# A recurrence in chunks and two feed-forward layers on one core: half 1's chunks in swapped rows, small products of both halves in turn, and one subtraction of layer 2 on VectorE

## The chip, the cores and the metric

The kernel runs as one program on one core of a Trainium2 chip. The metric is the device time of one execution in microseconds, smaller is better. Three executions of the kernel before were timed; one more was profiled.

## What is computed

The first part is a recurrence over 768 steps for 4 batches of 8 heads, with a state of 40 x 40 for each head; two feed-forward layers follow on its 3072 rows of 320 numbers.

```python
for t in range(768):
    y[t] = einsum('bhd,bhde->bhe', r[t], state)
    Sa = einsum('bhde,bhe->bhd', state, a[t])
    state = state * w[t][..., None] - einsum('bhd,bhe->bhde', Sa, b[t]) + einsum('bhd,bhe->bhde', v[t], k[t])
x = y as rows of 8 heads x 40                     # 3072 x 320
x = square(maximum(x @ w_in, 0)) @ w_out          # layer 1, 320 -> 2048 -> 320
h = x @ w_in2;  out = (h - tanh(h)) @ w_out2      # layer 2
```

All inputs and outputs are float32; the weights of the layers reach the chip as float64 bits and are converted there.

## The kernel before

**Attention.** The sequence is cut into 6 stretches of 128 steps, the batches into two pairs, so that there are 12 items k (`NT`). Of an item's two batches each is a half j (0 or 1). Inside the 128 steps there are two blocks (`blk`) of 64, and each block has two chunks (`c2`) of 32; c = 0..3 numbers the four chunks. Four pairs of heads lie beside each other in rows 0 to 39 and 64 to 103. `scalings` (L170) multiplies the decays up by scans on VectorE. `front` (L229) and `solve` (L292) build and invert the small triangular systems of two items at once on VectorE. `keys` (L259) transposes the scaled keys on TensorE, and ScalarE copies them from PSUM to `kbn`: a chunk takes 64 rows (32 of k, 32 of b), chunk 0 of a block rows 0 to 63 and chunk 1 rows 64 to 127.

`back` (L334) is the recurrence. For each chunk c, one after the other:

1. at a block's first chunk the state `zi` is transposed into `pz` (L393), 16 instructions (a float32 product shows as two instructions in the trace);
2. `pu` (L399): 8 products per half with 104 rows of contraction and 32 columns of the array, all 8 at columns `r0 = 64 * c2 + 32`, the same for both halves;
3. ScalarE writes -`pu` into the tile `vu` (L401), and copies `pz` to `zt` (L405);
4. `pd` (L423): 8 products per half from 64 rows `k0 = 64 * c2`, the outputs in turn in columns 0 to 39 and 64 to 103 (`par`);
5. VectorE adds `pd` to the state (L428, two instructions per half), at the last chunk it also multiplies by the decay (L430).

In steps 2 and 4 the source goes over half 0 first and then over half 1, each with a PSUM tile of its own. `result` (L435) makes the outputs from `vu`: transposed (L443), scores `pm` (L451) masked by a constant from `cst` (L454), and products with `kbn` and `zt` (L469, L472). `b_load` (L323) loads v into rows `64 * c2` and following of `vu`, and `v_load` (L164) loads v into `zi`.

**Layers.** `stream` (L726) runs 12 jobs of 256 rows for layer 1 and 12 for layer 2. A job has 8 steps m: 16 products into `hp` (L789), the activation, and 12 products into `acc` (L738: 8 with the high part `gh` of the activation, 4 with the low part `gl`), these up to 3 steps later. In layer 2, `act2` (L855) of step m issues on ScalarE a square, tanh, relu and square (L857 to L860), then `act2_end` of step m-1 on VectorE (L847, L848), then L863 and L864 of step m on VectorE, then `act2_round` (L850) of step m-1: `gh` on ScalarE (L852) and the subtraction `gl = d - gh` on GpSimd (L853). `split` (L706) prepares the next job's input on GpSimd (L710, L713, L714). Layer 1's own subtraction is on GpSimd as well (L817).

**What sets the order.** The parts are generators that `mix` (L521) walks along a model clock; `clk.run(...)` is what a piece is planned to take on TensorE and `L_E` what comes between two pieces. This gives the program order, and `urgent` gives `back` a higher priority (`HP_B`) than `front` and both a higher one than the layers. A scheduler of the framework then places the instructions on each engine by priority and modelled readiness; on the chip each engine keeps that order. Within one PSUM tile, products keep the order of the source. The attention's PSUM tiles share 4 buffers (`ps_a`), which layer 2 uses for `hp`.

Of the kernel before, what the change touches and what calls it, by code (L numbers as in the profile page):

```python
# [9 lines left out]
F32 = mybir.dt.float32  # L10
# [4 lines left out]
ACTF = mybir.ActivationFunctionType  # L15
ALU = mybir.AluOpType
# [7 lines left out]
C_LM, C_AM, C_ZERO, C_ID = 0, 32, 96, 224  # L24
# [33 lines left out]
def consts():  # L58
    c = np.zeros((128, NCONST), np.float32)
    c[:, C_ID:C_ID + 128] = np.eye(128)  # L60
    i = np.arange(128)
    c[:, C_LM:C_LM + 32] = i[None, :32] < i[:, None] % 32
    rows = (i // 64) * 32 + i % 32
    c[:, C_AM:C_AM + 64] = rows[:, None] < np.arange(64)[None, :]
    return c
# [23 lines left out]
class Attention:  # L89
# [169 lines left out]
    def keys(self, k, j):  # L259
# [4 lines left out]
        q = 2 * (k % 2) + j  # L264
        yield lambda: max(self.s_ready[k][j], self.y_ready[k - 2] - L_Y if k > 1 else 0)
        for blk in range(2):
            pt = self.ps.tile([128, 4, 104], F32, tag="a", name="pt")
            for pr in range(4):
                nc.tensor.transpose(pt[:, pr, :], kbf[0:P, pr, blk, :], self.id[0:P, 0:P])
# [53 lines left out]
    def b_load(self, k):  # L323
# [3 lines left out]
        for j in range(2):  # L327
            q = 2 * (k % 2) + j
            for c2 in range(2):
                (getattr(nc, Q_B) if k else nc.sync).dma_start(out=self.vu[j][64 * c2:64 * c2 + 32, :, :, :, 0:40], in_=vn[s, q, c2])  # L330
# [3 lines left out]
    def back(self, k):  # L334
# [48 lines left out]
        for c in range(4):  # L383
            blk, c2 = c // 2, c % 2
            yield max(ready)
            for j in range(2):
                q = 2 * (k % 2) + j
                zi, vu, zt, au = self.zi[q][:, c2], self.vu[j], self.zt[j], aus[j]
                if c2 == 0:
                    pz = self.ps.tile([128, 4, 40], F32, tag="a", name="pz")  # L390
                    for pr in range(4):
# [4 lines left out]
                r0 = 64 * c2 + 32  # L396
                pu = self.ps.tile([128, 8, 40], F32, tag="a", name="pu")
                for h in range(8):
                    nc.tensor.matmul(pu[r0:r0 + 32, h, :], lhsT=au[0:104, 4 * (h % 2) + h // 2, 32 * c:32 * c + 32],  # L399
                                     rhs=zi[0:104, h % 2, h // 2, :], start=True, stop=True, tile_position=(0, r0))  # L400
                nc.scalar.activation(out=vu[r0:r0 + 32, blk].rearrange("p a r d -> p (a r) d")[:, :, 0:40], in_=pu[r0:r0 + 32],  # L401
                                     func=ACTF.Copy, scale=-1.0)
                if c2 == 0:
                    for p0 in (0, 64):
                        nc.scalar.activation(out=zt[p0:p0 + 40, blk], in_=pz[p0:p0 + 40].rearrange("p a d -> p (a d)"), func=ACTF.Copy)  # L405
# [4 lines left out]
                clk.run(0.28)  # L410
                ready[j] = clk.t + L_E
                if c2:
                    self.u_ready[k][j][blk] = ready[j]
            yield max(ready)
            for j in range(2):
                q = 2 * (k % 2) + j
                vu, kbn, zi, wx = self.vu[j], self.kbn[q], self.zi[q], self.wx[2 * (k and (k - 1) % 3 + 1) + j]
                k0 = 64 * c2
                pd = self.ps.tile([128, 4, 40], F32, tag="a", name="pd")
                for pr in range(4):  # L420
                    for par in range(2):
                        hh = 4 * par + pr
                        nc.tensor.matmul(pd[64 * par:64 * par + 40, pr, :], lhsT=kbn[k0:k0 + 64, blk, 40 * hh:40 * hh + 40],  # L423
                                         rhs=vu[k0:k0 + 64, blk, pr, par, 0:40], start=True, stop=True)
# [6 lines left out]
                clk.run(0.4)  # L431
# [3 lines left out]
    def result(self, k):  # L435
# [12 lines left out]
        def scores(j, blk, vut):  # L448
            pm = self.ps.tile([128, 4, 2, 64], F32, tag="a", name="pm")
            for pr in range(4):  # L450
# [4 lines left out]
                                    in1=cst[:, None, C_AM:C_AM + 64].to_broadcast([128, 8, 64]), op=ALU.mult)  # L455
# [208 lines left out]
def attn_moe(ctx, tc, r, k, v, w, a, b, wakb, w0, rt, vn, vz, w_in1, w_out1, w_in2, w_out2, cst, out):  # L664
# [471 lines left out]
```

## Time and profile before

| what | us |
|---|---|
| three executions | 1388.30, 1394.27, 1395.91 |
| their median | 1394.27 |
| the profiled execution's own time | 1393.79 |
| its span from first to last instruction | 1391.6 |

Over the span TensorE is busy 1221.7 us (88%), VectorE 947.2 us (68%), ScalarE 830.0 us (60%), GpSimd 675.2 us (49%); the granted TensorE clock is 0.941 of full speed in the mean. Up to 105 us the inputs are loaded and the first items prepared. From there to some 985 us the attention's items and layer 1's jobs share TensorE, and from 985 us to the end layer 2 runs.

How to read the rows: PE is TensorE's products, PEld its weight loads, DVE VectorE, ACT ScalarE, POOL GpSimd, SP the engine that issues most transfers. A row of the timeline gives the start in us, the time until the last of its instructions ended in us, engine, line, operation, output<-inputs, shapes, count, and in brackets idle time before it and who ended it. Products overlap each other's ends, so the time that a run of them takes of TensorE is read from its start to the start of the next row, not from the second column. L12 is line 12 of the kernel.

### The profile page before, as it was taken

Reading aid. Unit: us, or ns where it says so; the run is one execution under the profiler, and the core shown is the slowest. Engines: PE = TensorE matmul, PEld = TensorE weight load, DVE = VectorE, ACT = ScalarE, POOL = GpSimd, SP = SyncE. Lnnn points to the kernel's source line nnn. Section 1 sums busy time; section 2 is a strip of 40 time slices with the busy share of each in tenths; the row PEclk is TensorE's granted clock in tenths of the full one; section 3 lists DMA queues with packets and bytes.
Section 4 is the critical chain, followed back from the end, with each engine's and each line's share of the span. In section 5 each row is a group of like instructions: output and inputs, shape, how many; then the busy total and the mean of one; then the engine's idle time right before and its main releaser. Section 6 shows DMA issues by size and latency. Waiting matters only on the chain.

```text
span 1391.6 us, 40716 instructions
## 1 busy us (share of the span) xinstructions
PE 1221.7 (88%) x16682; PEld 1136.5 (82%) x16682; DVE 947.2 (68%) x1812; ACT 830.0 (60%) x1768; POOL 675.2 (49%) x713
## 2 busy tenths in 40 slices
PE   1347778999799988999799999999899999999996
PEld 1246668888789877888788889999899999999995
DVE  7899785555854675356935671321269999999996
ACT  4364627574466736574465746544477777777785
POOL 5366534445444635245533643245555555555543
PEclk9986868989999988999999999999999999999999
DMA  6444544554545535454554534236920000000000
GB/s 159 114 122 143 157 150 136 154 171 137 163 138 164 170 103 161 133 157 132 160 159 134 159 103 147 85 110 217 391 72 19 24 31 22 22 22 22 22 11 22
DMA packets 94406, 164.12 MB, mean 118 GB/s; under 512 B 17696, under 2 KB 66272, under 8 KB 94212
## 3 DMA queue, kind: packets, MB, share of 16 engines
q1 hardware_dynamic: 65028, 124.02, 29.8%
q0 software_dynamic: 9600, 21.68, 5.1%
q10 hardware_dynamic: 19584, 15.74, 3.4%
q8 instruction: 134, 2.20, 0.7%
q14 instruction: 60, 0.49, 0.1%
HBM read 133.81 MB, written 27.53 MB: 116 GB/s over the span
## 4 chain that ended last, share of the span: by engine, by line
DVE 35%; PE 32%; issue 11%; ACT 10%; DMA 8%; POOL 4%; ACTq 0%; SPq 0%; POOLq 0%; DVEq 0%
DVE e L847 10%; PE hp L789 8%; PE acc L738 7%; DVE e L863 4%; DVE e L864 4%; PE pu L399 3%; DVE wx L192 3%; DMA raw<-in_moe_w_in_dram 2%; PE pd L423 2%; PE pm L451 2%; DVE inw L196 2%; PE pa L375 2%; ACT tbd L369 2%; DMA raw<-in_moe_w_out_dram 2%; DVE T L313 1%
## 5 line engine op out<-in xcount | busy, mean ns | idle before, releaser
L853 POOL TENSOR_TENSOR gl<-e,gh 128x512 fp32r<-128x512 f32 x96 | 144.3, 1504 | 180.5 <-ACT gh L852 178.3
L817 POOL TENSOR_TENSOR gl<-g,gh 128x512 fp32r<-128x512 f32 x96 | 127.0, 1323 | 177.4 <-ACT g L816 172.2
L789 PE MATMUL hp<-xh,wi 128*128 128x256 f32 x960 | 195.5, 299 | 12.3 <-ACT r L814 9.9
L789 PE MATMUL hp<-xh,wi2s 128*128 128x256 f32 x960 | 170.0, 278 | 1.7 <-DMA wi2s<-wi 1.7
L789 PEld LDWEIGHTS hp<-xh,wi 128*128 128x128 f32 x960 | 155.7, 202 | 15.7 <-ACT r L814 10.9
L847 DVE SCALAR_TENSOR_TENSOR e<-e,e 128x512 f32<-128x512 f32 x96 | 155.9, 1624 | 3.3
L738 PE MATMUL acc<-wo,gh 128*128 128x320 f32 x768 | 147.2, 327 | 3.1 <-DMA wo<-wo 2.8
L789 PEld LDWEIGHTS hp<-xh,wi2s 128*128 128x128 f32 x960 | 141.9, 188 | 1.9 <-DMA wi2s<-wi 1.9
L789 PE MATMUL hp<-xl,wi 128*128 128x256 f32 x576 | 134.9, 298 | 0.0
L738 PEld LDWEIGHTS acc<-wo,gh 128*128 128x128 f32 x768 | 121.5, 199 | 5.5 <-ACT gh L852 3.0
L428 DVE TENSOR_TENSOR zi<-pd,zi 40x160 f32<-40x160 f32 x192 | 61.8, 322 | 90.4 <-PE pd L423 86.0
L789 PE MATMUL hp<-xl,wi2s 128*128 128x256 f32 x576 | 120.7, 278 | 0.0
L852 ACT ACTIVATE gh<-e 128x512 fp32r<-128x512 f32 x96 | 60.8, 633 | 88.6 <-DVE e L848 86.4
L585 POOL TENSOR_TENSOR st<-hc,st 128x160 fp32r<-128x160 f32 (+3 forms) x72 | 51.6, 717 | 112.7 <-ACT st L584 82.3
L789 PEld LDWEIGHTS hp<-xl,wi 128*128 128x128 f32 x576 | 103.2, 203 | 0.7
L863 DVE TENSOR_TENSOR e<-hp,e 128x512 f32<-128x512 f32 x96 | 65.0, 677 | 54.4 <-ACT e L858 48.9
L476 POOL DMA_DIRECT2D yT<-yt x96 | 65.2, 682 | 71.9 <-DVE yt L475 69.7
L814 ACT ACTIVATE r<-hp 128x512 f32<-128x512 f32 x96 | 57.3, 597 | 66.7 <-PE hp L789 65.0
L789 PEld LDWEIGHTS hp<-xl,wi2s 128*128 128x128 f32 x576 | 94.5, 188 | 0.0
L578 DVE TENSOR_SCALAR hc<-hc 128x160 f32<-128x160 f32 (+3 forms) x78 | 29.2, 375 | 94.9 <-ACT hc L569 87.1
L848 DVE COPY_PREDICATED e<-e,e 128x512 f32<-128x512 int32 x96 | 89.6, 933 | 3.2
L399 PE MATMUL pu<-zi,au 104*32 104x40 f32 x1536 | 79.0, 209 | 11.1 <-DVE zi L428 8.4
(154 smaller groups left out, 3151.4 us busy)
## 6 DMA issues: line engine op xcount, KB each, us to landing
wo<-wo SPq DMA_DIRECT2D x96, 640.0 KB
inq<-in_wakb_dram SPq DMA_DIRECT2D x36, 240.0 KB
raw<-in_moe_w_in_dram SPq DMA_DIRECT2D x24, 256.0 KB
raw<-in_moe_w_out_dram SPq DMA_DIRECT2D x16, 320.0 KB
wo<-st ACTq DMA_DIRECT2D x32, 160.0 KB
wi<-st ACTq DMA_DIRECT2D x40, 128.0 KB
raw<-in_moe_w_out_dram SPq DMA_DIRECT2D x32, 160.0 KB
wo<-st ACTq DMA_DIRECT2D x64, 80.0 KB
```

The costliest lines, as they stand in the source:

```text
L399: nc.tensor.matmul(pu[r0:r0 + 32, h, :], lhsT=au[0:104, 4 * (h % 2) + h // 2, 32 * c:32 * c + 32], rhs=zi[0:104, h % 2, h // 2, :], start= ...
L428: nc.vector.tensor_tensor(out=zn, in0=pd[rows], in1=zi[rows, c2, par], op=ALU.add)
L476: getattr(nc, Q_Y).dma_start(out=self.yT[k].rearrange("(a r d) (b t) -> b r d a t", a=4, r=2, b=2)[j, par][:, :, t], in_=yt[rows])
L738: nc.tensor.matmul(acc[n][j], lhsT=g[:, i, 128 * j:128 * j + 128], rhs=w[:, p, i, :], start=(m == 0 and i == 0 and e == 0), stop=(m == 7 a ...
L789: nc.tensor.matmul(hp[:, h, :], lhsT=wt, rhs=xx, start=(e == 0), stop=(e == 7))
L814: nc.scalar.activation(out=r, in_=hp, func=ACTF.Relu)
L817: nc.gpsimd.tensor_tensor(out=gl, in0=g, in1=gh.bitcast(F32), op=ALU.subtract)
L847: nc.vector.scalar_tensor_tensor(out=u, in0=q, scalar=rest, in1=u, op0=ALU.add, op1=ALU.mult)
L848: nc.vector.copy_predicated(out=d, mask=v.bitcast(I32), data=u)
L852: nc.scalar.activation(out=gh, in_=d, func=ACTF.Copy)
L853: nc.gpsimd.tensor_tensor(out=gl, in0=d, in1=gh.bitcast(F32), op=ALU.subtract)
L863: nc.vector.tensor_tensor(out=d, in0=hp, in1=th, op=ALU.subtract)
```

## The change

It has two parts.

The first is in the attention. In half 1 the two chunks of a block change places in the 128 rows: `b_load` puts them at `64 * (c2 ^ j)`, the mask in `cst` gets a second version rolled by 64 rows, and `keys` of half 1 writes the two chunks to the other place: a transpose in place of which two products with the identity stand, one per 64 columns. In `back` the two halves' 8 `pu` products go into one PSUM tile and alternate, half 0 and half 1 in columns `r0[j] = 64 * (c2 ^ j) + 32`; the two halves' `pd` products alternate too, half 0 and half 1 from different 64 rows and, neighbour by neighbour, into different columns. ScalarE writes both halves' `vu` first and the `zt` copies afterwards; the model times in `clk.run` are other ones.

The second is in layer 2: the subtraction `gl` of `act2_round` is on VectorE in place of GpSimd.

```diff
-C_LM, C_AM, C_ZERO, C_ID = 0, 32, 96, 224
+C_LM, C_AM, C_ZERO, C_ID = 0, 32, 160, 288
@@ consts
+    c[:, C_AM + 64:C_AM + 128] = np.roll(c[:, C_AM:C_AM + 64], 64, axis=0)
@@ keys
-                nc.tensor.transpose(pt[:, pr, :], kbf[0:P, pr, blk, :], self.id[0:P, 0:P])
+                if j:
+                    for c in (0, 64):
+                        nc.tensor.matmul(pt[64 - c:128 - c, pr, :], lhsT=kbf[0:P, pr, blk, c:c + 64], rhs=self.id[0:P, 0:P], start=True, stop=True)
+                else:
+                    nc.tensor.transpose(pt[:, pr, :], kbf[0:P, pr, blk, :], self.id[0:P, 0:P])
@@ b_load
-                ...dma_start(out=self.vu[j][64 * c2:64 * c2 + 32, :, :, :, 0:40], in_=vn[s, q, c2])
+                ...dma_start(out=self.vu[j][64 * (c2 ^ j):64 * (c2 ^ j) + 32, :, :, :, 0:40], in_=vn[s, q, c2])
@@ back
-            for j in range(2):
-                q = 2 * (k % 2) + j
-                zi, vu, zt, au = self.zi[q][:, c2], self.vu[j], self.zt[j], aus[j]
-                if c2 == 0:
+            zis = [self.zi[2 * (k % 2) + j][:, c2] for j in range(2)]
+            if c2 == 0:
+                pzs = []
+                for zi in zis:
                     pz = self.ps.tile([128, 4, 40], F32, tag="a", name="pz")
+                    pzs.append(pz)
...
-                r0 = 64 * c2 + 32
-                pu = self.ps.tile([128, 8, 40], F32, tag="a", name="pu")
-                for h in range(8):
-                    nc.tensor.matmul(pu[r0:r0 + 32, h, :], lhsT=au[0:104, 4 * (h % 2) + h // 2, 32 * c:32 * c + 32],
-                                     rhs=zi[0:104, h % 2, h // 2, :], start=True, stop=True, tile_position=(0, r0))
-                nc.scalar.activation(out=vu[r0:r0 + 32, blk]..., in_=pu[r0:r0 + 32], func=ACTF.Copy, scale=-1.0)
+            pu = self.ps.tile([128, 8, 40], F32, tag="a", name="pu")
+            r0 = [64 * (c2 ^ j) + 32 for j in range(2)]
+            for h in range(8):
+                for j in range(2):
+                    nc.tensor.matmul(pu[r0[j]:r0[j] + 32, h, :], lhsT=aus[j][0:104, 4 * (h % 2) + h // 2, 32 * c:32 * c + 32],
+                                     rhs=zis[j][0:104, h % 2, h // 2, :], start=True, stop=True, tile_position=(0, r0[j]))
+            clk.run(0.4)
+            for j in range(2):
+                q, vu, zt = 2 * (k % 2) + j, self.vu[j], self.zt[j]
+                nc.scalar.activation(out=vu[r0[j]:r0[j] + 32, blk]..., in_=pu[r0[j]:r0[j] + 32], func=ACTF.Copy, scale=-1.0)
...
-            for j in range(2):
-                k0 = 64 * c2
-                pd = self.ps.tile([128, 4, 40], F32, tag="a", name="pd")
-                for pr in range(4):
-                    for par in range(2):
-                        hh = 4 * par + pr
-                        nc.tensor.matmul(pd[64 * par:64 * par + 40, pr, :], lhsT=kbn[k0:k0 + 64, blk, 40 * hh:40 * hh + 40],
-                                         rhs=vu[k0:k0 + 64, blk, pr, par, 0:40], start=True, stop=True)
+            pds = [self.ps.tile([128, 4, 40], F32, tag="a", name="pd") for _ in range(2)]
+            for pr in range(4):
+                for j, par in ((0, 0), (1, 1), (0, 1), (1, 0)):
+                    k0, hh = 64 * (c2 ^ j), 4 * par + pr
+                    nc.tensor.matmul(pds[j][64 * par:64 * par + 40, pr, :], lhsT=self.kbn[2 * (k % 2) + j][k0:k0 + 64, blk, 40 * hh:40 * hh + 40],
+                                     rhs=self.vu[j][k0:k0 + 64, blk, pr, par, 0:40], start=True, stop=True)
+            clk.run(0.5)
@@ scores
-                                    in1=cst[:, None, C_AM:C_AM + 64].to_broadcast([128, 8, 64]), op=ALU.mult)
+                                    in1=cst[:, None, C_AM + 64 * j:C_AM + 64 * j + 64].to_broadcast([128, 8, 64]), op=ALU.mult)
@@ act2_round
-        nc.gpsimd.tensor_tensor(out=gl, in0=d, in1=gh.bitcast(F32), op=ALU.subtract)
+        nc.vector.tensor_tensor(out=gl, in0=d, in1=gh.bitcast(F32), op=ALU.subtract)
```

## Rows read from the trace of the kernel before

**Rows 1.** Stretches: length; busy us of PE, PEld, DVE, ACT, POOL; granted clock; DMA.
```profile
105.00:245.00 140.00, 108.63 (x1976) 96.81 (x1969) 108.45 (x254) 72.58 (x171) 70.63 (x80) 0.74 0.48 146
...
815.00:985.00 170.00, 166.51 (x2491) 157.03 (x2489) 48.92 (x146) 88.93 (x184) 76.59 (x118) 1.00 0.47 152
...
1104.00:1392.00 288.00, 270.65 (x2002) 260.97 (x2000) 271.41 (x290) 208.82 (x378) 141.67 (x96) 0.99 0.07 22
```

**Rows 2.** Timeline of layer 2, two steps and one meeting with `split`.
```profile
1156.02 1.52 POOL L853 TENSOR_TENSOR gl<-e,gh 128x512 fp32r<-128x512 f32 x1 [2.15 <-ACT gh L852]
...
1156.42 1.67 DVE L847 SCALAR_TENSOR_TENSOR e<-e,e 128x512 f32<-128x512 f32 x1
...
1158.12 0.76 DVE L848 COPY_PREDICATED e<-e,e 128x512 f32<-128x512 int32 x1
...
1158.77 0.67 DVE L863 TENSOR_TENSOR e<-hp,e 128x512 f32<-128x512 f32 x1
...
1158.97 0.63 ACT L852 ACTIVATE gh<-e 128x512 fp32r<-128x512 f32 x1 [0.84 <-DVE e L848]
...
1159.37 0.68 DVE L864 TENSOR_TENSOR e<-e,e 128x512 f32<-128x512 f32 x1
...
1160.08 1.68 DVE L847 SCALAR_TENSOR_TENSOR e<-e,e 128x512 f32<-128x512 f32 x1
...
1165.33 1.75 POOL L713 TENSOR_TENSOR xl<-xraw,xh 128x512 fp32r<-128x512 f32 x1
...
1165.96 1.75 DVE L848 COPY_PREDICATED e<-e,e 128x512 f32<-128x512 int32 x1
```

**Rows 3.** L789's products by stretch (16 per step), layer 2 early and later.
```profile
1054.40:1104.40 50.00, 27.66 (x224) 26.89 (x224) 1.00 0.06 18
1104.40:1368.80 264.40, 140.08 (x1104) 135.84 (x1105) 1.00 0.07 23
```

**Rows 4.** Line L847 alone: ns min/median/max, first and last start.
```profile
L847 DVE SCALAR_TENSOR_TENSOR e<-e,e x96: 692/1670/2311, 992.4 to 1378.0; 128x512 f32<-128x512 f32 x96
```

**Rows 5.** Timeline of TensorE at the end.
```profile
1373.91 1.43 PE L738 MATMUL acc<-wo2s,gh 128*128 128x320 f32 x8 [1.18 <-ACT gh L852]
...
1377.54 1.44 PE L738 MATMUL acc<-wo2s,gh 128*128 128x320 f32 x8 [1.18 <-ACT gh L852]
```

**Rows 6.** Timeline of TensorE in the attention, small products.
```profile
569.67 0.50 PE L423 MATMUL pd<-vu,kbn 64*40 64x40 f32 x16
570.10 0.54 PE L443 MATMUL pvt<-idt,vu 128*104 128x128 f32 x3
...
576.82 0.51 PE L393 MATMUL pz<-idt,zi 104*40 104x40 f32 x16
577.26 0.76 PE L399 MATMUL pu<-zi,au 104*32 104x40 f32 x16
577.95 0.51 PE L393 MATMUL pz<-idt,zi 104*40 104x40 f32 x16
...
594.00 0.95 PE L345 MATMUL pw<-TT,lc 32*32 32x16 f32 x90
```

**Rows 7.** The same view at 412 us: two halves' `pd` back to back.
```profile
412.41 0.81 PE L423 MATMUL pd<-vu,kbn 64*40 64x40 f32 x32
413.15 0.65 PE L443 MATMUL pvt<-idt,vu 128*104 128x128 f32 x4
```

**Rows 8.** The same view at 615 us: eight transposes of `keys`.
```profile
614.80 0.88 PE L269 MATMUL pt<-idt,inq 104*128 104x104 f32 x8
615.51 0.49 PE L832 MATMUL pt<-idt,x 128*128 128x128 f32 x3
```

**Rows 9.** The chain that ended last, from 100 to 985 us, by line.
```profile
by line: PE hp L789 11.2%; PE acc L738 9.8%; issue 8.1%; PE pu L399 5.2%; DVE wx L192 3.7%; PE pd L423 3.4%; PE pm L451 3.3%; PE pa L375 3.2%; DVE inw L196 3.0%; ACT tbd L369 2.9%; DMA raw<-in_moe_w_out_dram 2.8%; PE pl L250 2.1%; PE pvt L4
```

**Rows 10.** Groups by line: count, busy us, mean ns, idle before and who ended it.
```profile
L428 DVE TENSOR_TENSOR zi<-pd,zi 40x160 f32<-40x160 f32 x192 | 61.8, 322 | 90.4 <-PE pd L423 86.0
...
L401 ACT ACTIVATE vu<-pu 32x320 f32<-32x320 f32 x96 | 40.9, 428 | 58.2 <-PE pu L399 55.9
```

More of the change, by code (lines that the diff above doesn't have):

```diff
@@ L329, in b_load @@
             for c2 in range(2):
-                (getattr(nc, Q_B) if k else nc.sync).dma_start(out=self.vu[j][64 * c2:64 * c2 + 32, :, :, :, 0:40], in_=vn[s, q, c2])
+                (getattr(nc, Q_B) if k else nc.sync).dma_start(out=self.vu[j][64 * (c2 ^ j):64 * (c2 ^ j) + 32, :, :, :, 0:40], in_=vn[s, q, c2])
             for par in range(2):
@@ L395, in back @@
                     clk.run(0.46)
-                r0 = 64 * c2 + 32
-                pu = self.ps.tile([128, 8, 40], F32, tag="a", name="pu")
-                for h in range(8):
-                    nc.tensor.matmul(pu[r0:r0 + 32, h, :], lhsT=au[0:104, 4 * (h % 2) + h // 2, 32 * c:32 * c + 32],
-                                     rhs=zi[0:104, h % 2, h // 2, :], start=True, stop=True, tile_position=(0, r0))
-                nc.scalar.activation(out=vu[r0:r0 + 32, blk].rearrange("p a r d -> p (a r) d")[:, :, 0:40], in_=pu[r0:r0 + 32],
-                                     func=ACTF.Copy, scale=-1.0)
+            pu = self.ps.tile([128, 8, 40], F32, tag="a", name="pu")
[7 more added lines that the diff above has]
+                q, vu, zt = 2 * (k % 2) + j, self.vu[j], self.zt[j]
+                nc.scalar.activation(out=vu[r0[j]:r0[j] + 32, blk].rearrange("p a r d -> p (a r) d")[:, :, 0:40], in_=pu[r0[j]:r0[j] + 32],
+                                     func=ACTF.Copy, scale=-1.0)
+                ready[j] = clk.t + L_E
+                if c2:
+                    self.u_ready[k][j][blk] = ready[j]
+            for j in range(2):
+                q, zt = 2 * (k % 2) + j, self.zt[j]
                 if c2 == 0:
                     for p0 in (0, 64):
-                        nc.scalar.activation(out=zt[p0:p0 + 40, blk], in_=pz[p0:p0 + 40].rearrange("p a d -> p (a d)"), func=ACTF.Copy)
+                        nc.scalar.activation(out=zt[p0:p0 + 40, blk], in_=pzs[j][p0:p0 + 40].rearrange("p a d -> p (a d)"), func=ACTF.Copy)
                 if c < 2:
@@ L409, in back @@
                     self.v_load(s + 1, q, c - 2)
[L410 to L413, printed above, removed]
             yield max(ready)
+            pds = [self.ps.tile([128, 4, 40], F32, tag="a", name="pd") for _ in range(2)]
[5 more added lines that the diff above has]
+            clk.run(0.5)
             for j in range(2):
                 q = 2 * (k % 2) + j
-                vu, kbn, zi, wx = self.vu[j], self.kbn[q], self.zi[q], self.wx[2 * (k and (k - 1) % 3 + 1) + j]
-                k0 = 64 * c2
-                pd = self.ps.tile([128, 4, 40], F32, tag="a", name="pd")
-                for pr in range(4):
-                    for par in range(2):
-                        hh = 4 * par + pr
-                        nc.tensor.matmul(pd[64 * par:64 * par + 40, pr, :], lhsT=kbn[k0:k0 + 64, blk, 40 * hh:40 * hh + 40],
-                                         rhs=vu[k0:k0 + 64, blk, pr, par, 0:40], start=True, stop=True)
+                zi, wx, pd = self.zi[q], self.wx[2 * (k and (k - 1) % 3 + 1) + j], pds[j]
                 for par in range(2):
@@ L430, in back @@
                         nc.vector.tensor_tensor(out=zn, in0=zn, in1=wx[rows, :, 128:129].to_broadcast([40, 4, 40]), op=ALU.mult)
-                clk.run(0.4)
                 ready[j] = clk.t + L_E
```

## The prediction

> **What bounds the kernel now.** I read the busy time by stretch first, then the timeline and the chain of waits inside two stretches, because the two parts of the change lie in stretches with different limits.
>
> In layer 2, from 1104 us on, VectorE is busy 271 of 288 us [rows 1]. A step's VectorE work starts every 3.66 us, and L847 alone takes 1.67 us of it. The timeline shows why: GpSimd's `gl` begins at 1156.02, L847 at 1156.42, and L847 ends only 0.55 us after `gl` does; L848 stretches from 0.76 to 1.75 us where it meets `split` [rows 2]. Alone, L847 takes 0.69 us [rows 4]. So VectorE stands still while GpSimd reads. TensorE is close behind: between 1054 and 1104 us, where it works off what it had in store, 224 products of `hp` (14 steps) pass in 50.0 us, 3.57 us a step; from 1104 on 1104 products (69 steps) take 264.4 us, 3.83 us a step [rows 3]. VectorE with GpSimd sets 3.83, TensorE's own floor is 3.57.
>
> From 815 to 985 us TensorE is busy 166.5 of 170 us at full clock; from 105 to 245 us it has gaps and a granted clock of 0.74 [rows 1], between the two levels of 1.2 and 2.4 GHz in turn. On the chain from 100 to 985 us `pu` has 5.2% and `pd` 3.4% [rows 9], that is 46 and 30 us. The rows of TensorE's timeline give their price: sixteen `pu` instructions hold it from 577.26 to 577.95, 0.69 us; sixteen of `pz`, with the same 104 rows but two groups of columns in turn, from 576.82 to 577.26, 0.44 us; sixteen of `pd`, also in two groups of columns, 0.43 us [rows 6]. Column groups in turn overlap; `pu`, all in one group, cannot.
>
> **Layer 2's subtraction, -22 us.** GpSimd loses one instruction per step, VectorE gets one. Without GpSimd beside it, VectorE's step is, from start to start, L863 0.60, L864 0.60 to 0.71, L848 0.65 [rows 2], L847 0.7 [rows 4], and `gl`, an operation of two SBUF inputs of 128x512 like L864, 0.6 to 0.7: 3.15 to 3.36 us. That is under TensorE's 3.57, so the bound moves to TensorE. `split` still meets VectorE once in 8 steps and can add about 1 us in each of its three instructions (1.75 in place of 0.76), 3 us per job; the room is 8 x (3.57 - 3.15), 3.4 us, or 1.7 us at the dearer end, and two more steps are buffered in `hp`. The 69 steps from 1104 us give 69 x (3.83 - 3.57) = 18 us. At the end the last `acc` runs wait for `gh` and start 3.63 us apart [rows 5] where 12 products need 1.75; with a shorter VectorE chain I take 4 us of some 5.6 to be had. What is queued behind the new instruction: `gl` of step m-1 waits on VectorE for `gh`, and L847 of step m waits behind it; `gh` follows L860 on ScalarE, just as L864 does, so the wait is covered by L864. Bounds: 6 us if `split` and the dearer step leave VectorE at 3.74, 24 us with the whole end.
>
> **The attention's products, -20 us.** Per item four chunks with two halves make 96 runs of `pu` before, and 48 double runs after.
> - `pu`: 96 x 0.69 = 66 us before. Two column groups in turn cost for 32 instructions what two halves' `pd` cost back to back, 412.41 to 413.15, 0.74 us [rows 7]: 48 x 0.74 = 36 us. Gain 31 us; nothing at the other end. I take 31, since `pz` has the same rows, and since both halves share one PSUM tile, whose products keep their order.
> - `pd`: 96 x 0.43 = 41 us. They already overlap in pairs. Four regions in turn might come near the small `pw`, 90 in 0.95 us [rows 6], 0.34 for 32: a gain up to 25 us. But half 0's `vu` is ready 0.43 us before half 1's [rows 10], and the two tiles of `pd` may be issued apart as now: nothing. I take 4, near that end, the price of fewer runs.
> - `keys`: eight transposes hold TensorE 0.71 us [rows 8], 0.09 each. Half 1's 4 per block (24 blocks) become 8 float32 products, 16 instructions of the same length: two at a time 0.72 us in place of 0.36, 24 x 0.36 = 9 us lost; 26 us if they do not overlap. I take 9, as `pz` overlaps.
> - `b_load`, the mask and 64 more columns of constants move the same bytes or nearly, and the same DMAs; `zt` behind both `vu` on ScalarE and `v_load` behind it on SP cost nothing while `pd` and its sums run over 1 us. If that cover is gone, one ScalarE copy of 0.43 us per chunk, 21 us in all, would show.
>
> Together 31 + 4 - 9 = 26 us of TensorE at full clock, 28 with the stretches below it. Of `pu` and `pd` about 0.7 lies on the chain (46 of 66, 30 of 41 us), the rest beside waits for VectorE's scans and loads that stay: 0.7 x 28 = 20 us. Bounds: 40 us gained (all of it, with some of `pd`'s regions) to 5 us lost.
>
> The sum against the profiled execution: 1393.8 - 22 - 20 = 1352 us. That execution is 0.5 us under the median of the runs shown, so the same number stands for the median.
>
> The trace has column groups overlapping with equal rows [rows 6]. The Trainium skill, "TensorE: Matmul & The Clock Gate", section "What overlaps and what doesn't", says otherwise: a weight load overlaps products in flight only when their row group differs, and both halves' `pu` have the same rows. By that rule `pu` would gain nothing and the sum would be 1394 - 22 + 3 = 1375; here the trace disagrees with it.
>
> **The rivals.**
> 1. The attention gains nothing: the scheduler issues the halves apart, or waits for the later half eat it. That is also how the change would not do what it says. For it: the gaps before 245 us [rows 1], and VectorE's sums wait 90 us for `pd` [rows 10]. Time 1394 - 22 = 1372. Chance 0.20.
> 2. Equal rows do not overlap after all: `pu` stays at 66 us and `keys` adds up to 9, on the chain by less than half. Against it: `pz`. Time 1375. Chance 0.04.
> 3. All of TensorE's saved time and part of `pd`'s regions reach the end: 1394 - 22 - 36 = 1336. For it: no gaps from 815 us on. Chance 0.08.
> 4. The new `gl` stalls VectorE: if VectorE waits for the whole 0.63 us of `gh` [rows 2] in each step, VectorE's step is back at 3.8 and only the end and the attention pay, 1394 - 17 = 1377. Against it: L864 covers it. Chance 0.04.
> 5. Slower: the halves in lockstep. Every chunk now waits for both halves' sums and copies, 2 x 0.32 + 0.43 us more [rows 10], and where that misses its place in the order, for a quarter step of a layer (0.9) as well, less the 0.76 us of shorter runs (0.64 of `pu`, 0.12 of `pd`): 1.2 us in each of 48 chunks, 58 us. Time 1394 - 22 + 58 = 1430. It decides from (22 + 7) / 48 = 0.6 us a chunk. Against it: layer 1's products fill TensorE's waits, so lockstep costs nothing while there is filling. Chance 0.07; at half its price it cancels the gain to within 7 us, chance 0.06.
>
> **How the numbers follow.** My forecast, both parts paying, has 0.51, its own range 1340 to 1366; rivals 1 to 4 have 0.36, all under 1378. About 0.5%, 7 us, is what a measurement of this kernel can tell from no change, so faster is 0.87, same 0.06, slower 0.07. The range 1334 to 1379 takes in the forecast, rivals 1, 2 and 4 and the slow half of rival 3, and leaves out the lockstep.
>
> **What would show it.** Right: in layer 2 a step of TensorE every 3.57 us to the end, L847 at 0.7 us, TensorE without waits for `gh`. In the attention: `pu` in 48 runs of 32 of about 0.74 us, half 1's `pt` runs of 16 at about 0.72 us, layer 2 beginning some 20 us sooner. Wrong: L847 short but a step still above 3.7 us (rival 4); `pu` runs of 1.4 us (rival 2); `pu` at 0.74 us but layer 2 beginning where it did, with more idle time of TensorE before `pu` and `pd` (rivals 1 and 5). A different order of the whole schedule, which one edit can cause, would make it wrong without any of these.

## The result and the profile after

The changed kernel takes 1328.07 us (median of four executions, 1324.36 to 1332.29); the kernel before, run beside it, 1391.28 us (1382.47 to 1395.91). The ratio is 0.955, 95% interval 0.949 to 0.962; the medians lie 63 us apart. The forecast was 1352 us; the direction was right, and the time lies 6 us under the range's lower end. The profiled execution took 1324.36 us with a span of 1322.6 us. In all ratios of this study slow executions are left out, which bears on two of the kernel before (1397.50 and 1401.33 us) beside the last four runs of the table below.

The whole span first: engine shares of the changed kernel.

```profile
PE 1164.2 (88%) x16970; PEld 1091.7 (83%) x16970; DVE 914.9 (69%) x1908; ACT 833.1 (63%) x1768; POOL 532.1 (40%) x617
```

TensorE's share is what it was, 88%, with 57.5 us less of busy time. The same stretches as in [rows 1], columns as there; the last stretch is shorter because the kernel ends at 1322.6, and layer 2's first product comes at 946.7 us in place of 979.4, inside the second.

```profile
105.00:245.00 140.00, 110.20 (x2062) 95.67 (x2053) 112.93 (x263) 76.16 (x177) 76.94 (x85) 0.82 0.52 157
815.00:985.00 170.00, 167.44 (x2185) 159.37 (x2184) 51.73 (x96) 96.06 (x189) 79.90 (x123) 0.98 0.54 187
1104.00:1323.00 219.00, 210.99 (x1645) 210.46 (x1643) 196.95 (x294) 171.23 (x307) 21.77 (x18) 0.99 0.07 23
```

In the last stretch VectorE is no longer the busiest engine: 197 of 219 us against TensorE's 211, where before it had 271 of 288 against 271 [rows 1]. The timeline of VectorE in layer 2 shows the step, to be held against [rows 2] (L865 is the new `gl`, L859, L860, L875 and L876 are L847, L848, L863 and L864 of before):

```profile
1152.83 0.69 DVE L876 TENSOR_TENSOR e<-e,e 128x512 f32<-128x512 f32 x1 [0.30 <-ACT e L872]
1153.44 0.68 DVE L865 TENSOR_TENSOR gl<-e,gh 128x512 fp32r<-128x512 f32 x1
1154.05 0.68 DVE L859 SCALAR_TENSOR_TENSOR e<-e,e 128x512 f32<-128x512 f32 x1
1154.77 0.77 DVE L860 COPY_PREDICATED e<-e,e 128x512 f32<-128x512 int32 x1
1155.42 0.68 DVE L875 TENSOR_TENSOR e<-hp,e 128x512 f32<-128x512 f32 x1
1156.40 0.69 DVE L876 TENSOR_TENSOR e<-e,e 128x512 f32<-128x512 f32 x1 [0.30 <-ACT e L872]
...
1164.76 1.31 DVE L859 SCALAR_TENSOR_TENSOR e<-e,e 128x512 f32<-128x512 f32 x1
1166.11 1.75 DVE L860 COPY_PREDICATED e<-e,e 128x512 f32<-128x512 int32 x1
```

A step is 1156.40 - 1152.83 = 3.57 us, with 0.30 us of waiting in it and no wait for `gh` before L865. L859 alone, as in [rows 4], and L865 (ns min/median/max):

```profile
L859 DVE SCALAR_TENSOR_TENSOR e<-e,e x96: 669/685/1315, 959.5 to 1311.3; 128x512 f32<-128x512 f32 x96
```
```profile
L865 DVE TENSOR_TENSOR gl<-e,gh x96: 673/686/2595, 963.8 to 1313.4; 128x512 fp32r<-128x512 f32 x96
```

0.685 us in place of 1.67; in these rows an operation is stretched only beside `split` (1164.76 and 1166.11 above; `split` is on GpSimd from 1164.70 on). Layer 2's products, as in [rows 3]: 896 of them, 56 steps, from 1104.40 to 1305.70, where the last step's products start, 3.59 us a step in place of 3.83.

```profile
1104.40:1305.70 201.30, 110.66 (x896) 107.72 (x897) 1.00 0.07 23
```

The end of TensorE's timeline, as in [rows 5]:

```profile
1307.52 1.33 PE L750 MATMUL acc<-wo2s,gh 128*128 128x320 f32 x8
...
1309.28 1.33 PE L750 MATMUL acc<-wo2s,gh 128*128 128x320 f32 x8
...
1311.04 1.33 PE L750 MATMUL acc<-wo2s,gh 128*128 128x320 f32 x8
...
1313.45 1.44 PE L750 MATMUL acc<-wo2s,gh 128*128 128x320 f32 x8 [0.49 <-ACT gh L864]
```

The last runs follow each other every 1.76 us and wait once, 0.49 us. From the start of the last step's `hp` products to the end the kernel takes 1322.6 - 1305.7 = 16.9 us; before it was 1391.6 - 1368.9 = 22.7.

The attention's small products in the same view, as in [rows 6 to 8]:

```profile
536.65 0.52 PE L432 MATMUL pd<-vu,kbn 64*40 64x40 f32 x32
537.09 0.71 PE L750 MATMUL acc<-wo,gl 128*128 128x320 f32 x3
...
549.74 0.77 PE L407 MATMUL pu<-zi,au 104*32 104x40 f32 x32
550.44 0.57 PE L240 MATMUL pt<-idt,inq 104*128 104x104 f32 x4
...
592.82 0.93 PE L272 MATMUL pt<-idt,inq 104*64 104x104 f32 x16
593.59 0.59 PE L399 MATMUL pz<-idt,zi 104*40 104x40 f32 x22
```

From start to next start, 32 `pu` instructions take 0.70 us (before, 16 took 0.69); 32 of `pd` take 0.44 (before 0.74 [rows 7]); 16 of half 1's `keys` take 0.77 (before, 4 transposes about 0.36).

### The profile page after: what moved, and what is told of

It is laid out like the page before. It is cut to its first block, busy times and chain, and to the rows that moved or that the text cites. A ratio compares the mean times of both kernels' runs of the same rounds, so it can differ in the third digit from the quotient of the medians.

```text
span 1322.6 us, 41123 instructions
## 1 busy us (share of the span) xinstructions
PE 1164.2 (88%) x16970; PEld 1091.7 (83%) x16970; DVE 914.9 (69%) x1908; ACT 833.1 (63%) x1768; POOL 532.1 (40%) x617
## 4 chain that ended last, share of the span: by engine, by line
PE 52%; DVE 15%; ACT 7%; DMA 6%; issue 4%; SPq 1%; ACTq 0%; POOL 0%; DVEq 0%; POOLq 0%
PE hp L801 19%; PE acc L750 13%; PE accb L750 6%; DMA raw<-in_moe_w_out_dram 3%; PE pm L463 2%; PE pd L432 2%; PE pa L380 2%; DVE wx L193 2%; PE pu L407 2%; DVE inw L197 2%; DMA raw<-in_moe_w_in_dram 1%; DVE T L318 1%; PE py L481 1%; ACT tbd L374 1%; PE pw L350 1%
## 5 line engine op out<-in xcount | busy, mean ns | idle before, releaser
L829 POOL TENSOR_TENSOR gl<-g,gh 128x512 fp32r<-128x512 f32 x96 | 128.5, 1338 | 159.3 <-ACT g L828 149.9
L801 PE MATMUL hp<-xh,wi 128*128 128x256 f32 x960 | 187.1, 292 | 2.3 <-ACT xt L847 2.3
L801 PE MATMUL hp<-xh,wi2s 128*128 128x256 f32 x960 | 167.2, 276 | 1.5 <-POOL xh L722 1.5
L801 PEld LDWEIGHTS hp<-xh,wi 128*128 128x128 f32 x960 | 149.4, 195 | 7.8 <-ACT xt L847 2.9
L722 POOL CAST xh<-xraw 128x768 fp32r<-128x768 f32 x24 | 20.1, 838 | 266.3 <-PE hp L801 238.5
L801 PEld LDWEIGHTS hp<-xl,wi 128*128 128x128 f32 x576 | 100.2, 196 | 1.3 <-issue 0.2
L590 DVE TENSOR_SCALAR hc<-hc 128x160 f32<-128x160 f32 (+3 forms) x78 | 34.0, 437 | 96.7 <-ACT hc L581 94.0
L875 DVE TENSOR_TENSOR e<-hp,e 128x512 f32<-128x512 f32 x96 | 65.3, 680 | 42.8 <-ACT e L870 42.7
L869 ACT ACTIVATE e<-hp 128x512 f32<-128x512 f32 x96 | 57.3, 597 | 49.5 <-PE hp L801 45.1
L860 DVE COPY_PREDICATED e<-e,e 128x512 f32<-128x512 int32 x96 | 86.3, 898 | 2.8
L380 PE MATMUL pa<-tbd,rhs 128*104 128x128 f32 x384 | 57.8, 313 | 30.4 <-ACT tbd L374 30.1
L380 PEld LDWEIGHTS pa<-tbd,rhs 128*104 128x104 f32 x384 | 53.0, 200 | 34.1 <-ACT tbd L374 33.2
```

What stands on the lines that cost most here:

```text
L380: nc.tensor.matmul(pa[0:104, i, :], lhsT=self.rhs[q][:, i, 40 * g:40 * g + 104], rhs=self.tbd[:, 4 * g + i, :], start=True, stop=True)
L590: (nc.gpsimd if self.count in self.pool_clamps else nc.vector).tensor_scalar(out=hc, in0=hc, scalar1=F64_LOW, scalar2=F64_HIGH, op0=ALU.ma ...
L801: nc.tensor.matmul(hp[:, h, :], lhsT=wt, rhs=xx, start=(e == 0), stop=(e == 7))
L829: nc.gpsimd.tensor_tensor(out=gl, in0=g, in1=gh.bitcast(F32), op=ALU.subtract)
L860: nc.vector.copy_predicated(out=d, mask=v.bitcast(I32), data=u)
L869: nc.scalar.activation(out=s, in_=hp, func=ACTF.Square)
```

## The experiments

**Where the time is saved: the two parts alone.** `gl_only` is the kernel before with the subtraction on VectorE; `attn_only` is the changed kernel with the subtraction back on GpSimd.

```diff
@@ gl_only (in the kernel before); attn_only is the reverse line in the changed kernel
-        nc.gpsimd.tensor_tensor(out=gl, in0=d, in1=gh.bitcast(F32), op=ALU.subtract)
+        nc.vector.tensor_tensor(out=gl, in0=d, in1=gh.bitcast(F32), op=ALU.subtract)
```

> The kernel before with layer 2's subtraction on VectorE and nothing else. Theory: the subtraction explains all that layer 2 gained, its first steps included: steps of 3.57 us to the end (22 us), a shorter end (6 us) and some 9 us among the first dozen steps, where GpSimd no longer has both layers' subtractions in its queue: about 36 us less, near 1355 us, and the part up to layer 2's first product as long as before (979 us). Rival: the first steps gained because the attention's new order left the weight loads earlier; then about 28 us less, near 1363 us, and from the first product to the thirteenth step 75 us as before.

> The changed kernel with layer 2's subtraction back on GpSimd: the attention's part alone. Theory: it shortens the part ahead of layer 2 by about 33 us and nothing behind, near 1358 us, and layer 2's steps are at 3.83 us again. Rival: it also shortens layer 2's first steps, near 1350 us. If the two parts hinder or help each other, the gains of this run and of the subtraction alone don't add up to the 63 us of both.

All runs of this study in one table, in four groups of four runs. Medians are of four executions; the ratio is against the kernel before, timed beside each group, and is not the ratio of the two medians. The medians of the kernel before were 1391.05, 1388.48, 1392.43 and 1387.06 us in the four groups.

| run | median us | ratio, 95% interval |
|---|---|---|
| gl_only | 1367.35 | 0.987, 0.981 to 0.992 |
| attn_only | 1353.88 | 0.975, 0.970 to 0.980 |
| pu_apart | 1351.37 | 0.974, 0.967 to 0.982 |
| pd_apart | 1323.38 | 0.956, 0.949 to 0.962 |
| no_swap | 1344.97 | 0.968, 0.964 to 0.971 |
| keys_both | 1354.36 | 0.976, 0.973 to 0.980 |
| keys_host | 1338.57 | 0.964, 0.960 to 0.968 |
| plan_before | 1350.76 | 0.974, 0.971 to 0.976 |
| gl_plan_new | 1367.90 | 0.985, 0.977 to 0.993 |
| gl_plan_near | 1367.90 | 0.984, 0.977 to 0.992 |
| plan_less | 1339.61 | 0.963, 0.957 to 0.970 |
| plan_more | 1334.88 | 0.960, 0.953 to 0.966 |
| pu_apart_less | 1358.21 | 0.978, 0.970 to 0.987 |
| pu_apart_more | 1347.73 | 0.974, 0.967 to 0.982 |
| pd_apart_less | 1327.61 | 0.961, 0.952 to 0.970 |
| pd_apart_more | 1331.77 | 0.961, 0.952 to 0.969 |

By the medians the subtraction alone saves 24 us, the attention's part alone 37 us; together 61, and both at once 63. By the means it is 21 and 36, and 62 for both. The intervals reach some 8 us to either side, so the parts add up as far as these runs tell. For `gl_only` both theory and rival had expected more, 36 and 28 us. To see where the time was saved, each trace is cut where layer 1's last relu starts (1016.9, 1009.6, 977.9 and 974.4 us). The busy time by stretch, columns as in [rows 1], of the kernel before:

```profile
105.00:1016.90 911.90, 832.50 (x13301) 762.46 (x13294) 509.39 (x1242) 509.42 (x1156) 433.26 (x527) 0.92 0.51 155
1016.90:1391.60 374.70, 355.73 (x2655) 345.59 (x2653) 347.02 (x371) 272.21 (x495) 188.97 (x130) 1.00 0.08 24
```

of `gl_only`:

```profile
1009.60:1361.00 351.40, 343.68 (x2676) 343.07 (x2674) 317.26 (x468) 276.80 (x499) 43.33 (x36) 0.99 0.08 27
```

of `attn_only`:

```profile
105.00:977.90 872.90, 792.45 (x13524) 726.14 (x13525) 504.23 (x1241) 510.70 (x1155) 436.43 (x526) 0.91 0.52 162
977.90:1353.40 375.50, 354.20 (x2642) 343.67 (x2640) 346.22 (x369) 271.08 (x493) 187.64 (x130) 0.99 0.08 24
```

and of the changed kernel:

```profile
105.00:974.40 869.40, 787.44 (x13537) 721.18 (x13528) 507.86 (x1246) 511.34 (x1157) 436.43 (x525) 0.93 0.53 163
974.40:1322.60 348.20, 339.83 (x2642) 339.10 (x2640) 314.39 (x462) 272.89 (x493) 41.93 (x36) 1.00 0.08 25
```

The second stretch goes from 374.7 to 351.4 with the subtraction alone, and from 375.5 to 348.2 on top of the attention's part: 23 and 27 us. The first stretch goes from 911.9 to 872.9 with the attention's part alone, 39 us. The cut is good to a few us only, since layer 2 begins ahead of it: in `gl_only` the first stretch, 904.6 us long, is 7 us shorter as well. Read length minus PE busy there: TensorE stands still for 79.4 us before, 80.5 us in `attn_only`, 82.0 us after. In these three the waits hardly shrank or grew; busy time fell by 40 us and the stretch by 39.

Which products? The groups of TensorE's products by line from 105 to 1016.9 us (busy us, mean ns, idle before), of the kernel before:

```profile
L399 PE MATMUL pu<-zi,au 104*32 104x40 f32 x1504 | 77.4, 209 | 10.6 <-DVE zi L428 8.4 <-ACT lc L253 1.0 <-ACT zt L405 0.6
L451 PE MATMUL pm<-rt,vut 104*128 104x128 f32 x384 | 64.7, 318 | 5.7 <-ACT vut L444 2.8 <-issue 2.2 <-ACT zt L405 0.6
L423 PE MATMUL pd<-vu,kbn 64*40 64x40 f32 x1504 | 53.7, 210 | 4.2 <-DVE rhs L254 3.1 <-ACT vu L401 1.1
L250 PE MATMUL pl<-inq 40*32 40x64 f32 x1152 | 32.3, 226 | 0.9 <-DVE zi L428 0.7
```

and of `attn_only`:

```profile
L463 PE MATMUL pm<-rt,vut 104*128 104x128 f32 x384 | 54.5, 291 | 1.0 <-issue 1.0
L407 PE MATMUL pu<-zi,au 104*32 104x40 f32 x1502 | 45.9, 212 | 5.3 <-issue 2.1 <-ACT st L596 1.3 <-DVE zi L441 1.3
L432 PE MATMUL pd<-vu,kbn 64*40 64x40 f32 x1504 | 44.5, 213 | 7.9 <-ACT vu L412 5.5 <-issue 1.5 <-DVE rhs L255 0.9
L251 PE MATMUL pl<-inq 40*32 40x64 f32 x1152 | 26.0, 227 | 4.4 <-ACT vu L412 2.3 <-issue 1.2 <-DVE zi L441 0.8
```

In these rows the product count is the same but for two missing records, and one product's mean duration hardly changes in the small ones; what shrinks is the time that a run covers. `pu` loses 31.5 us and `pd` 9.2; `keys` (the same view: 21.2 to 29.7) gains 8.5. Beyond these, `pm` loses 10.2 and `pl`, with its second group, 7.0, `pz` 2.8, while `pw` gains 4.9 and `py` 5.9, though the change touches none of them. These times overlap at the ends, so they only come near a sum. Counted over the two windows from each product's start to the next, as prices are read here, `pu` loses 29.5 us, `pd` 8.4, `keys` gain 10.8: -27 us. The five others together lose 8.4, and all the rest (layer 1's products and `front`'s transposes for the most part) 5: -40 us, the busy time of the windows.

**What each interleaving is worth.** `pu_apart` and `pd_apart` are the changed kernel with one group of products in the old order, half 0 first; rows, tiles and counts stay.

```diff
@@ pu_apart
-            for h in range(8):
-                for j in range(2):
+            for j in range(2):
+                for h in range(8):
@@ pd_apart
-            for pr in range(4):
-                for j, par in ((0, 0), (1, 1), (0, 1), (1, 0)):
+            for j, pr in ((j, pr) for j in range(2) for pr in range(4)):
+                for par in range(2):
```

> The changed kernel, with the pu products of half 0 ahead of those of half 1 in place of in turn, still in one PSUM tile and in the changed columns. Theory: each half's eight products sit in one group of columns again, 1.3 us a chunk in place of 0.70, 30 us of TensorE, of which 0.7 reaches the end: about 20 us slower than the change, near 1348 us. Rival as above: no slower than 1332 us.

> The changed kernel, with the pd products of half 0 ahead of those of half 1 in place of in turn; rows and columns stay as changed. Theory: four regions of the array worked at once, so 32 pd instructions go from 0.45 us back to 0.74 to 0.86 us, 15 to 20 us of TensorE over 48 chunks, of which 0.7 reaches the end: 10 to 14 us slower than the change, near 1340 us. Rival: the gain ahead of layer 2 comes from the new order and not from TensorE's time; then no slower than 1332 us.

TensorE's timeline of `pu_apart`, then of `pd_apart`:

```profile
553.91 1.22 PE L407 MATMUL pu<-zi,au 104*32 104x40 f32 x32
555.06 0.53 PE L251 MATMUL pl<-inq 40*32 40x64 f32 x22
```
```profile
545.46 0.69 PE L432 MATMUL pd<-vu,kbn 64*40 64x40 f32 x32
546.08 0.76 PE L251 MATMUL pl<-inq 40*32 40x64 f32 x52
```

Both runs are longer, as expected: `pu` 1.15 us in place of 0.70, `pd` 0.62 in place of 0.44. By 48 runs that would be 22 us and 9 us of TensorE. The times say 23 us slower for `pu`, and 5 us faster, not slower, for `pd`. One kernel each doesn't settle the second, since an edit also changes the order of everything else; the next groups are about that.

**The swapped rows and the keys.** `no_swap` takes the swap out and leaves the interleaved source (both halves' `pu` again in the same columns, in two tiles). `keys_both` makes half 0's keys by two products as well, in their own places. `keys_host` has half 1's keys swapped already in the inputs, so that both halves are transposed as before (half 1's scaling becomes two VectorE instructions).

```diff
@@ no_swap (b_load, mask and transposes as in the kernel before)
-            r0 = [64 * (c2 ^ j) + 32 for j in range(2)]
+            r0 = [64 * c2 + 32 for j in range(2)]
@@ keys_both
-                if j:
-                    for c in (0, 64):
...
+                for c in (0, 64):
+                    r = 64 - c if j else c
+                    nc.tensor.matmul(pt[r:r + 64, pr, :], lhsT=kbf[0:P, pr, blk, c:c + 64], rhs=self.id[0:P, 0:P], start=True, stop=True)
@@ keys_host (layout of the inputs; readers of kb use chunk c ^ j)
+    kb[:, 1::2] = kb[:, 1::2][:, :, :, :, :, [1, 0, 3, 2]].copy()
```

> The changed kernel without the swapped rows: both halves' products are still issued in turn and copied together, but half 1's chunks stay where half 0's are (so pu of both halves in one group of columns and in two PSUM tiles, pd of both from the same 64 rows), and the keys of both halves are transposes. Theory: pu costs 1.15 us a chunk in place of 0.70, pd some 0.74 in place of 0.45, the keys 8 us less in all: 22 + 3 to 14 - 8, so 17 to 28 us slower than the change, 1345 to 1356 us. Rival, that the joint issue and not the overlap in the array brought the gain: no slower than 1335 us.

> The changed kernel, in which half 0's keys too are made by two products per transpose (in their own places), so that the price of that edit stands twice. Theory: the part ahead of layer 2 is as long as TensorE's occupied time plus waits that don't change, so its time passes one to one: 8 to 9 us slower than the change, near 1336 us. Rival, the share of 0.7 or less that the prediction took: 0 to 6 us, under 1334 us.

> The changed kernel with half 1's keys in transposes again: the inputs are laid out with half 1's chunks of k and b in swapped places already, the products of front read them crosswise, and the scaling on VectorE takes two instructions in place of one for half 1. Theory: TensorE gets its 8 to 9 us back and the time falls by as much, near 1319 us. Rival: the keys' products lie beside other waits; then 1324 to 1330 us.

Without the swap 17 us are lost. But `no_swap` is also 22 us faster than `gl_only`, although its `pu` still covers 75.6 us and its keys cost what they did before (the view by line). So joining the two halves' products in one step of the source may be worth something by itself; this is one order of each kernel, and 22 us is no more than an order alone can do (next group). Where it could come from, the rows of `pm` show, from 105 to 1022 us, of `gl_only` and then of `no_swap`:

```profile
L451 PE MATMUL pm<-rt,vut 104*128 104x128 f32 x384 | 62.2, 309 | 2.5 <-ACT vut L444 1.1 <-issue 0.8 <-ACT zt L405 0.5
```
```profile
L459 PE MATMUL pm<-rt,vut 104*128 104x128 f32 x384 | 53.2, 288 | 0.0
```

The same 384 products come in 52 runs in `gl_only` (counted in TensorE's timeline), in 38 in `no_swap` and in 40 in the changed kernel: fewer foreign products fall between. In the fourteen kernels with joined halves `pm` covers 52 to 57 us, in the four with separate ones 58 to 65; `pl` (with its second group) 27 to 35 us and 31 to 39. Joining isn't the only way to that: `gl_plan_new` (next group) has separate halves and other model times, and there `pm` comes in 34 runs and covers 58.2 us.

The two runs on the keys can't be read as prices: `keys_both` loses 26 us where the keys' products grow by 8 us (31.6 to 39.8 us busy), and `keys_host` loses 10 us where they shrink to 21 us, at the price of one more VectorE instruction per item in half 1's scaling. Up to layer 1's last relu `keys_both` is 26 us longer than the changed kernel: TensorE is busy for 15 us more and stands still for 11 us more (92.9 against 82.0). So something else moves by ten or twenty us with an edit.

**The order of the schedule.** These runs change only the model times behind the two groups of products, `clk.run(0.4)` after `pu` and `clk.run(0.5)` after `pd`. No instruction is added or left out; only their order can change. `plan_before` doubles what one half had in the kernel before.

```diff
@@ plan_before (plan_less: 0.38, 0.48; plan_more: 0.44, 0.56)
-            clk.run(0.4)
+            clk.run(0.56)
...
-            clk.run(0.5)
+            clk.run(0.8)
@@ gl_plan_new, in gl_only (gl_plan_near: 0.29, 0.41)
-                clk.run(0.28)
+                clk.run(0.2)
...
-                clk.run(0.4)
+                clk.run(0.25)
```

> The changed kernel with the model times of the kernel before for pu and pd (0.56 and 0.80 per chunk of both halves in place of 0.40 and 0.50), which only moves where the order puts the layers' products. Theory: the order's plan doesn't carry the gain; within 6 us of the change, 1322 to 1334 us. Rival, that the plan carried part of it: over 1336 us.

> The kernel before with the subtraction on VectorE and, in its own separate products, the changed model times (pu 0.20 and pd 0.25 per half in place of 0.28 and 0.40). It does nothing of the attention's change on the array. Theory 1, that the shorter plan itself brings part of the attention's gain: 8 to 20 us under the subtraction alone (1367 us), so 1347 to 1359 us. Theory 2, that the products' overlap brings it, and that a plan is only good or bad luck of the order: 1360 to 1375 us.

> The kernel before with the subtraction on VectorE and model times moved by almost nothing (0.29 and 0.41 in place of 0.28 and 0.40). It measures how much the order alone can do: if the time stays within 4 us of 1367 us, orders of one and the same work are alike; if it moves by 8 us or more in either direction, differences of that size between kernels of other orders prove nothing about their parts.

> The changed kernel with model times a little shorter (0.38 and 0.48 in place of 0.40 and 0.50). The same question on the changed side: within 4 us of 1328 us if orders are alike; if the change's own order is a lucky one, 1335 to 1350 us, as with the kernel before's model times (1351 us).

> The changed kernel with model times a little longer (0.44 and 0.56). Within 4 us of 1328 us if orders are alike; 1335 to 1350 us if the change's own order is a lucky one; and if a longer plan by itself costs time, between the change and the 1351 us of 0.56 and 0.80, near 1336 us.

The changed kernel takes 1339.6, 1328.1, 1334.9 and 1350.8 us at four sets of model times: 23 us of scatter from order alone. The kernel with only the subtraction takes 1367.4, 1367.9 and 1367.9 at three. So the attention's part is worth 28, 40, 33 or 17 us against 1367.7, mean 29, and the change's own times are the best of the four. In these seven runs the new structure's time reacts more to its order than the old one's; more sets might show otherwise. Equal times don't mean that the order did nothing, though: up to layer 1's last relu `gl_plan_new`'s TensorE is busy for 13 us less than `gl_only`'s (815.8 and 828.8 us) and stands still for 15 us more (91.0 and 75.8).

Where the scatter lies shows in part. The first stretch of `plan_before`, to its last relu of layer 1:

```profile
105.00:995.60 890.60, 812.92 (x13548) 746.31 (x13540) 510.61 (x1247) 510.68 (x1159) 433.51 (x525) 0.91 0.51 159
```

It is 21 us longer than the changed kernel's. TensorE is idle for 77.7 us there and 82.0 in the changed kernel, so it isn't waits; the same work is 25 us more busy. The rows of `pd` and `pw` from 105 to 1022 us, of the changed kernel and then of `plan_before`:

```profile
L432 PE MATMUL pd<-vu,kbn 64*40 64x40 f32 x1504 | 45.2, 213 | 11.8 <-ACT vu L412 7.9 <-issue 2.2 <-DVE rhs L255 0.9
L350 PE MATMUL pw<-TT,lc 32*32 32x16 f32 x1408 | 27.7, 191 | 5.9 <-issue 4.4 <-DVE gate L325 1.5
```
```profile
L432 PE MATMUL pd<-vu,kbn 64*40 64x40 f32 x1504 | 54.1, 219 | 9.3 <-ACT vu L412 8.3 <-DVE rhs L255 0.9
L350 PE MATMUL pw<-TT,lc 32*32 32x16 f32 x1408 | 36.7, 198 | 1.7 <-DVE lc L323 1.7
```

Each covers 9 us more. The scheduler lets the two alternate more often in this order: TensorE goes from `pd` to `pw` 90 times in place of 55 (counted in the timeline). From start to start that is 13 of the 25 us; what such an alternation takes is shown below. The mean granted clock is a little lower, 0.91 against 0.93, but it doesn't carry the scatter: `attn_only`, with 0.91 as well, has a stretch of 872.9 us, and the four executions of the changed kernel, with clocks of 0.954, 0.953, 0.939 and 0.957 over the whole span, took 1324.4, 1330.7, 1325.5 and 1332.3 us. Nor is it alternation everywhere: `plan_less` has 44 switches and is 11.5 us slower than the change; there TensorE stands still for 93.2 us.

**Both interleavings again, at three orders.** With scatter of this size `pu` and `pd` were compared at the sets of `plan_less` and `plan_more` too.

> pu of half 0 ahead of half 1's, with the model times 0.38 and 0.48. The changed kernel at these times took 1340 us. Theory, that pu's overlap in the array is worth 20 us of TensorE whatever the order: 1352 to 1368 us, and the mean over the three plans some 20 us over that of the changed kernel. Rival, that its 23 us were the order's luck: the mean within 8 us.

> The same with the model times 0.44 and 0.56. The changed kernel at these times took 1335 us. Theory: 1347 to 1363 us; the rival: 1330 to 1343 us.

> pd of half 0 ahead of half 1's, with the model times 0.38 and 0.48; the changed kernel took 1340 us. Theory, that pd's overlap between the halves is worth its 0.17 us per chunk, some 8 us, and that the lack of a loss at the change's own times was the order's luck: 1340 to 1354 us, the mean over three plans 4 to 10 us over the changed kernel's. Rival, that pd's turns are worth nothing: the mean within 3 us or below.

> The same with the model times 0.44 and 0.56; the changed kernel took 1335 us. Theory: 1336 to 1350 us; the rival: 1328 to 1338 us.

| model times | changed | pu apart | pd apart |
|---|---|---|---|
| 0.38, 0.48 | 1339.6 | 1358.2 (+18.6) | 1327.6 (-12.0) |
| 0.40, 0.50 | 1328.1 | 1351.4 (+23.3) | 1323.4 (-4.7) |
| 0.44, 0.56 | 1334.9 | 1347.7 (+12.8) | 1331.8 (-3.1) |
| mean | 1334.2 | 1352.4 (+18.3) | 1327.6 (-6.6) |

`pu`'s turns are worth 18 us, near the 22 us of TensorE that they save, with one sign at every order. For `pd`'s turns between the halves no gain shows, although each whole run is shorter by 0.18 us; the sign is against them at all three orders, though at two of them by less than the spread of a kernel's own executions (8 us in the changed kernel). One reason shows in the rows of `pd`: in turn it covers 44.4, 45.2 and 47.5 us, apart 46.7, 46.1 and 48.6 (from 105 to 1022 us, the orders as in the table). That is 1 to 2 us saved and not 9; 40 to 44 of the 48 double runs stay whole, and in turn the rest falls into more pieces. It doesn't explain a loss. Another thing was seen that goes that way: the scheduler sometimes lets `pd` and `pw` alternate. TensorE's timeline in `pu_apart`, whose `pd` is that of the changed kernel:

```profile
585.09 0.27 PE L432 MATMUL pd<-vu,kbn 64*40 64x40 f32 x2
585.28 0.24 PE L350 MATMUL pw<-TT,lc 32*32 32x16 f32 x2
585.45 0.27 PE L432 MATMUL pd<-vu,kbn 64*40 64x40 f32 x2
```

Such a pair takes 0.36 us, while two `pd` instructions in a run of their own take 0.03. Switches from `pd` to `pw` number 55 in the changed kernel and 38 in `pd_apart`. 17 pairs of some 0.3 us are 5 us. But at the other two orders the counts are 44 and 41, and 58 and 54, and it is with 3 switches fewer that `pd_apart_less` is 12 us faster. So the count doesn't carry the difference, and the cause stays open.

## Why the prediction was wrong

- **What bounds it**: as read. VectorE with GpSimd set layer 2's step at 3.83 us, and with the subtraction moved the step is TensorE's, 3.59 us against the 3.57 foreseen [rows 2 to 4].
- **Layer 2's subtraction, -22**: measured -24 by the medians, -21 by the means. The step is 3.59 us to the last product, and the end gave 5.8 us where 4 was taken. `gl` follows L864's counterpart L876 without a wait in the rows above: rival 4 fell.
- **`pu`, -31**: measured -29.5 from start to start, and a whole run of 0.70 us where 0.74 was taken. The price came from `pd` [rows 7], and `pz` [rows 6] rightly told that equal rows overlap. Rivals 1 and 2 fell. By the Trainium skill, "TensorE: Matmul & The Clock Gate", section "What overlaps and what doesn't", a load overlaps products in flight only in another row group. By that, turns between two column groups with equal rows would gain nothing; 32 `pu` instructions take 0.70 us in turn and 1.15 us apart, so it doesn't hold here.
- **`pd`, -4**: a term mis-sized within its bounds; TensorE is held 8.4 us less. Not much of that comes from the turns between the halves: with them undone `pd` covers only 1 to 2 us more. And an order alone can do nearly as much: by the rows from 105 to 1022 us `pd` covers 54.2 us in `gl_only` and 47.4 in `gl_plan_new`, both with the products of the kernel before.
- **`keys`, +9**: measured +10.8 from start to start. The three terms together are -27 us, against 28 taken: the sum of TensorE's time was right.
- **The share of 0.7: a step that failed.** I took 28 us of TensorE time and let 0.7 of it through, by the share of `pu` and `pd` that lay on the chain [rows 9], the rest to vanish beside waits for scans and loads. But TensorE's idle time was 79, 80 and 82 us before, with the attention's part, and after: what was saved in busy time was saved in the stretch, 40 and 39 us. With the share at 1 and the measured -24 the sum is 1393.8 - 24 - 28, or 1342 us, so this step makes some 8 of the 24 us that the forecast missed. Rival 3 had this mechanism, at too low a chance. That idle time stays is no rule, though: over the runs here it lies between 71 us (`no_swap`) and 93 (`plan_less`, `keys_both`), and `pu`'s turns, compared at three orders, pass 18 of some 22 us.
- **A term put at nothing: the other step that failed.** The sum had no effect of the change on products that it doesn't touch. In `attn_only` these take 13 us less from start to start: `pm`, `pl` and `pz` come in fewer and longer runs, `pw` and `py` take more, layer 1's products a little less. No run tells how much of that is the joining of the halves and how much the order that came with it. All let through, -27 and -13 give -40 and 1393.8 - 24 - 40 = 1330 us, against 1328 measured; that is an account of one trace, not a second forecast.
- **The order**: named as a way to be wrong, but with no width in the range. It moved the changed kernel by up to 23 us without a single instruction changed, and the order that the change came with is the best of the four tried. Over the four, the attention's part is worth 29 us in the mean, so some 10 of the 40 us at the change's own times belong to that order. The mean of the four, 1338 us, lies inside the range: that the time fell below it is in part luck.
- **Lockstep (rival 5)**: idle time ahead of `pu` and `pd` together was 14.8 us before, 13.2 us in `attn_only` (the groups above) and 18.1 us in the changed kernel; of the 58 us feared nothing is to be seen.

What stays open: why `pd` apart is no slower or even faster, what the keys cost in time, what joining the halves is worth by itself, and what in an order makes TensorE wait or split its runs. `pd_apart` is a candidate for a faster kernel, 1323.4 against 1328.1 us, and lower at three orders out of three; at any one order that isn't clear of the scatter.

## What to carry to other kernels

Where one engine has the only long queue and other work is ready to fill its gaps, the share of an operation on the chain of waits can be the wrong factor: ask whether the engine's idle time would change, and if not, let the whole saving through. Here it stayed in three versions, and moved by some 10 us in others. When a scheduler places the instructions, time the same kernel at a few sets of model times before reading a difference of 1 to 2% as the price of an edit; a part whose effect keeps its sign and size over them, as `pu`'s turns did, is far better shown than by one run. In this kernel small products gained from taking turns between two column groups (1.15 to 0.70 us for 32 `pu` instructions); check by a run's start to the next start, as busy time per instruction doesn't show it. And check the sum over the whole kernel as well: `pd`'s whole runs became shorter by 0.18 us, its total by 1 to 2 us.

## What was not expected of the hardware

- 32 `pd` instructions with two row groups and two column groups in turn take 0.44 us, 14 ns each, against 0.62 us in `pd_apart`, where each half's 16 have two column groups alone: the row groups overlap as well.
- An alternation of `pd` (64 rows, 40 columns) with `pw` (32 rows, 32 columns), two instructions of each, takes 0.36 us, about as long as 26 `pd` instructions in a run of their own.
- VectorE's L847 took 1.67 us beside GpSimd's subtraction and, as L859 of the changed kernel, 0.685 us without it, with operands of the same shape. What the subtraction takes on GpSimd alone no run shows.
